# A recurrent loop fed by streamed weights: homes for resident weights opened earlier, the ring filled ahead of the loop, kept outputs stored by partition

## The chip, the cores and the metric

The kernel runs on one core of a Trainium2 chip. The metric is the device time of one execution in microseconds. Three executions of the kernel before took 2130.72, 2140.69 and 2147.24 us; their median is 2140.69 us. A fourth execution was profiled.

## What is computed

Two independent results stand side by side in the output, columns 0 to 1023 (part A) and 1024 to 2047 (part B), both over 2048 rows in bfloat16.

```python
# A: a short causal convolution, a product, a long convolution by FFT, a gate
k_shift = sum(k_pad[:, t:t + S, :] * shift_k[:, ks - 1 - t] for t in range(ks))   # ks = 4
kv = k_shift * v
y = irfft(rfft(kv, 2 * S) * rfft(ssm_k, 2 * S))[:, :S, :] + kv * ssm_D
a = q * y
# B: attention with a recurrent memory, 64 segments of 32 rows, H = 32 heads of 128, M = 8
mem = mem0
for s in range(64):
    h = concatenate([mem, x[:, 32 * s:32 * s + 32]], axis=1)        # 40 rows
    q, k, v = h @ Wq, h @ Wk, h @ Wv                                # [32 heads, 40, 128]
    p = softmax(where(mask, q @ k.T * scale, -1e9))
    o = (p @ v) @ Wo
    mem = o[:, :8]                                                  # into the next segment
    outs.append(o[:, 8:])
```

Each segment needs all of Wq, Wk, Wv and Wo (8 MB each, 32 MB together), which is more than SBUF holds, and needs the memory rows that the segment before it has put out.

## The kernel before, in words

**Order.** Everything is written in one function under a manual schedule: each engine carries out its instructions in the order in which the program gives them. Most transfers are issued by SP, in order, and an SP instruction that waits holds up all that stand behind it; others are issued by ACT and by POOL.

**Part A** is a four-step transform. Stage 1 (to line 510) makes SK1 and SU1 in DRAM. Stage 2 (lines 513 to 620) runs a software pipeline over 17 sets x 2 halves, index `i` from -1 to 34: `load_set` gathers a set of K and U from DRAM, two sets ahead, into buffers of the pool `gio` (three of each); `unit_k`, `unit_u`, `unit_prod` and `unit_back` work on them; `scatter` stores the result to SZ. Stage 3 (lines 623 to 653) takes 16 tiles `t`: it loads `zt` from SZ and `qt`, two tiles ahead, multiplies on PE into `y_ps`, and DVE multiplies by `qt` into `ot`, which SP stores. `ot` has two buffers.

**The row work of part B.** Of the 40 rows of a segment, the last 8 are not touched by the recurrence when q, k and v are formed. The class `Rows` does their projections for all segments at once, in between part A's work, as 192 half steps of four matmuls: 12 units (q, k and v of four head groups) of eight pieces each. A piece is one half, 256 KB, of a weight pair. `rows.load_to(n)` issues the loads of pieces up to n, into the pair's lasting home if it has one (`res_half`), and otherwise into one of the eight tiles of `pring`. Results are gathered in `stq` (q and k, stored to QKBd by ACT after each k unit) and `stv` (v, stored to VBd by POOL).

**Weights.** The 64 pairs [128, 2, 1024] (512 KB each) are 45 resident ones, 2 that are parked in PSUM (`park`, copied to a ring tile in each segment), and 17 that are streamed in each segment through a ring of five tiles (`wring`). Resident homes are opened pool by pool with `open_res(n)` as space comes free, in the order of first use: 9, 10, 3, 12, 2, and the last 9 just ahead of the loop. The Wo pairs come last in that order: 2 of the 11 resident ones are loaded ahead of the loop, 9 in segment 0 (`first_loads`). The streamed pairs of q, k and o are first copied from DRAM to DRAM into a contiguous form, Wst, by `relay` on POOL: ten in stage 2, two after stage 3.

**The loop** (lines 912 to 995) takes the 64 segments one after the other. `qk_part` and `v_part` project the 32 rows that depend on the memory, `tr_a`, `scores`, `softmax`, `blocks` and `pv` are the attention of one head group, and `wo` the projection that gives `yacc`. When PE is done with a streamed pair, `done` issues the load of the one that is five places ahead (`place`). The attention results of the last 8 rows of each segment, OL, aren't needed by the recurrence; POOL stores them to OLd in DRAM, 64 KB for a segment. In the last segment they are loaded back, into the place of early weights (`Wearly`, as `OLs`), after `wo(u0)`, and behind the loop lines 1000 to 1015 project them with all of Wo: four blocks (`sh`, `rq`) of 256 matmuls, each evicted half by ACT and half by DVE and stored by SP.

**Between stage 3 and the loop** (lines 654 to 706) come: `load_h(0)`, the rest of the pieces, the four parked halves (`park_w`, through `pring`; two rounds of transposes each), the two Wo pairs, the two late relays, the rest of the row work from half step 162 on, the closing of the pools of the row work (`cp`), and only then the pool of the ring, with the first five `place()`.

Of the kernel before, what the change touches and what calls it, by code (L numbers as in the profile page):

```python
# [21 lines left out]
def fused_kernel(ctx: ExitStack, tc, q, k, v, shift_k, ssm_k, ssm_D, outa, x, mem0, Wq, Wk, Wv, Wo, outb, n_seg):  # L22
# [11 lines left out]
    nc = tc.nc  # L34
# [16 lines left out]
    QKBd = dram.tile([4, 128, n_seg * 128], BF, name="QKBd")  # L51
    OLd = dram.tile([n_seg, 128, 256], BF, name="OLd")
    VBd = dram.tile([4, 4, n_seg, 8, 256], BF, name="VBd")
# [30 lines left out]
    cp = ExitStack()  # L84
    stq = cp.enter_context(tc.tile_pool(name="b_stq", bufs=1, side="right"))
    stv = cp.enter_context(tc.tile_pool(name="b_stv", bufs=1, side="right"))
    hb = cp.enter_context(tc.tile_pool(name="b_hb", bufs=1, side="right"))
    hTB = hb.tile([128, 8, n_seg * 8], BF, name="hTB")
    pring = cp.enter_context(tc.tile_pool(name="b_pring", bufs=8, side="right"))
    ps_p = cp.enter_context(tc.tile_pool(name="b_ps_p", bufs=2, space=PSUM, side="right"))  # L90
# [422 lines left out]
    with ExitStack() as c2:  # L513
        gio = c2.enter_context(tc.tile_pool(name="a2_io", bufs=3, side="right"))
        wk = c2.enter_context(tc.tile_pool(name="a2_wk", bufs=2, side="right"))
        ps_u = c2.enter_context(tc.tile_pool(name="a2_psu", bufs=2, space=PSUM))
        ps_k = c2.enter_context(tc.tile_pool(name="a2_psk", bufs=2, space=PSUM))
# [85 lines left out]
        for i in range(-1, len(hs) + 1):  # L603
            if 0 <= i < len(hs):
                st, hf = hs[i]
                if hf == 0:
                    load_set(st + 2)
                    zs_of[st] = wk.tile([128, 2, 1024], BF, tag="zs", name="zs", bufs=3)
            if i + 1 < len(hs):
                K_[i + 1] = unit_k(*hs[i + 1])  # L610
            if 0 <= i < len(hs):
                Y_[i] = unit_prod(*hs[i], K_[i], U_[i])
            rows.half(1)
            if i >= 1:
                unit_back(*hs[i - 1], Y_[i - 1], zs_of[hs[i - 1][0]])
            if i + 1 < len(hs):
                U_[i + 1] = unit_u(*hs[i + 1])
            if i >= 16 and i % 2 == 0:
                relay(1)
    ca2.close()  # L620


    with ExitStack() as c3:
        io = c3.enter_context(tc.tile_pool(name="a3_io", bufs=3, side="right"))
        wk = c3.enter_context(tc.tile_pool(name="a3_wk", bufs=2, side="right"))
        ps_big = c3.enter_context(tc.tile_pool(name="a3_ps", bufs=3, space=PSUM))
        open_res(12)
        zts = {}

        def load_z(t):  # L630
            if t < 16:
# [4 lines left out]
                zts[t] = zt, qt  # L636

        load_z(0)
        load_z(1)
        rows.load_to(rows.at // 16 * 8 + 16)  # L640
        rows.go(4)
        for t in range(16):
            load_z(t + 2)
            rows.half(4 if t < 6 else 1)
            zt, qt = zts[t]
            pt = ps_big.tile([128, 1024], F32, tag="big", name="y_ps")
            for hf in range(2):
                for h in range(2):
                    nc.tensor.matmul(pt[:, hf * 512:(hf + 1) * 512], lhsT=G2h[h][:, :],
                                     rhs=zt[:, h, hf * 512:(hf + 1) * 512], start=(h == 0), stop=(h == 1))  # L650
            ot = wk.tile([128, 1024], BF, tag="ot", name="ot")
            nc.vector.tensor_tensor(out=ot[:], in0=pt[:], in1=qt[:], op=ALU.mult)
            nc.sync.dma_start(rows_view(outa, t), ot[:])
    ca.close()
    open_res(2)
    act = cw_.enter_context(tc.tile_pool(name="b_act", bufs=1))
    act2 = cw_.enter_context(tc.tile_pool(name="b_act2", bufs=2))
    n_o = [key for key in resident if key[0] == "o" and key in res_pool]

    def load_h(s):  # L660

        H_ = act.tile([128, 256], BF, tag="qks", name="H")
        if s == 0:
            nc.gpsimd.dma_start(H_[0:32, :], mem0.rearrange("t (dq c) -> (t dq) c", dq=4))
            nc.gpsimd.dma_start(H_[32:128, :], x[0:24].rearrange("t (dq c) -> (t dq) c", dq=4))
        else:
            nc.scalar.dma_start(H_[:], x[32 * s - 8:32 * s + 24].rearrange("t (dq c) -> (t dq) c", dq=4))
        return H_

# [6 lines left out]
    park_s = stv.tile([128, 4, 1024], BF, tag="stv", name="park_s")  # L676
    halves = [(key, n) for key in parked for n in range(2)]
    assert rows.at >= 160
    rows.load_to(96)
    park_w = []  # L680
    for key, n in halves:
        park_w.append(pring.tile([128, 1024], BF, tag="pring", name="park_w"))
        nc.sync.dma_start(park_w[-1][:], half_src(key, n))
    for key in n_o:
        for n in range(2):
            res_half(key, n)
    relay(len(relaid))
    rows.half(6, "AD")
    for i, (key, n) in enumerate(halves):
# [5 lines left out]
        for c in range(8):  # L695
            nc.tensor.transpose(park[key][n][:, c * 128:(c + 1) * 128], park_s[:, i, c * 128:(c + 1) * 128], ident[:])
    while rows.at < 192:
        rows.half(2, "AD")
    assert len(rows.loaded) == 96
    cp.close()  # L700
    ring = cw_.enter_context(tc.tile_pool(name="b_ring", bufs=RING, reuse_waits="tile"))
    open_res(len(to_open))

    pp = ExitStack()
    ps_a = pp.enter_context(tc.tile_pool(name="b_ps_a", bufs=3, space=PSUM))
    ps_ts = pp.enter_context(tc.tile_pool(name="b_ps_ts", bufs=1, space=PSUM))

    placed = {}
    to_copy = []
    todo = [key for s in range(n_seg) for key in streamed if key[0] != "o" or s < n_seg - 1]  # L710

    def place():

        if todo:
            key = todo.pop(0)
            t = ring.tile([128, 2, 1024], BF, tag="wring", name="wring")
            nc.sync.dma_start(t[:], Wst[key])
            placed.setdefault(key, []).append(t[:])

# [6 lines left out]
    def pair(key):  # L726
        return res[key][:, :, :] if key in res else placed[key].pop(0)

# [32 lines left out]
    def qk_out(u):  # L761
        u.qks = act.tile([128, 512], BF, tag="qks", name="qks")
        nc.scalar.copy(u.qks[:], u.qk[:])  # L763
# [23 lines left out]
    def tr_a(u):  # L787
        tp = transposes(u.qks)
        tv = tp[:].rearrange("e (j t c r) -> e t c j r", j=4, t=2, c=2)
        QK = act.tile([128, 8, 72], BF, tag="qks", name="QK")  # L790
        u.QT, u.KT = QK[:, :, 0:32], QK[:, :, 32:72]
# [4 lines left out]
    def load_b(s):  # L796
        qkb = act.tile([128, 4, 128], BF, tag="qkb", name="qkb")
        nc.sync.dma_start(qkb[:], QKBd[:, :, s * 128:(s + 1) * 128].rearrange("g e x -> e g x"))
        return qkb
# [58 lines left out]
    def pv(u, s):  # L858
# [11 lines left out]
        if u.g == 3 and s + 1 < n_seg:  # L870
            nc.gpsimd.dma_start(OLd[s], OL[:].rearrange("e h r -> e (h r)"))

# [29 lines left out]
    def new_hT():  # L902
        return act.tile([128, 8, 32], BF, tag="hT", name="hT")

    for _ in range(RING):
        place()
    load_vb(0)
    qkb = load_b(0)
    n_o = [key for key in resident if key[0] == "o" and key not in n_o]
    hT = new_hT()  # L910
    h_rows(H, hT, 0)
    for s in range(n_seg):
        last = s + 1 == n_seg
        def first_loads(g):
            for key in (n_o[3 * g:3 * g + 3] if s == 0 else ()):
                for n in range(2):
                    res_half(key, n)
# [25 lines left out]
        if last:  # L943
            spare = [key for key in resident if key[0] != "o" and key[1] < 1 + (key[0] == "qk") and key not in early]
            for key, at in zip([key for key in streamed if key[0] == "o"], spare):
                nc.sync.dma_start(res[at][:], Wst[key])
                res[key] = res[at]
        qk_part(u2, range(4, 8))
        qk_out(u2)
# [24 lines left out]
        wo(u0, Y)  # L974
        if last:
            for s0, s1 in ((0, 32), (32, s)):
                nc.sync.dma_start(OLs[:, s0:s1].rearrange("e s h r -> e s (h r)"),
                                  OLd[s0:s1].rearrange("s e x -> e s x"))
        pv(u2, s)
# [20 lines left out]
    for sh in range(2):  # L1000
        for rq in range(2):
            pl = ps_l.tile([128, 1024], F32, tag="pl", name="pl")
            for h in range(32):
                w = pair(("o", h // 8, h % 8 // 2))[:, h % 2, :]
                for hf in range(2):
                    for r in range(4):
                        nc.tensor.matmul(pl[32 * r:32 * r + 32, hf * 512:(hf + 1) * 512],  # L1007
                                         lhsT=OLs[:, 32 * sh:32 * sh + 32, h, 4 * rq + r],
                                         rhs=w[:, hf * 512:(hf + 1) * 512], start=(h == 0), stop=(h == 31),
                                         tile_position=(0, 32 * r))  # L1010
            ol = ring.tile([128, 2, 1024], BF, tag="wring", name="ol")
            nc.scalar.copy(ol[:, 0, 0:512], pl[:, 0:512])
            nc.vector.tensor_copy(ol[:, 0, 512:1024], pl[:, 512:1024])
            for r in range(4):
                nc.sync.dma_start(outl[24 + 4 * rq + r, 32 * sh:32 * sh + 32, :], ol[32 * r:32 * r + 32, 0, :])
    msched.__exit__(None, None, None)
# [67 lines left out]
```

## Time and profile before

| | us |
|---|---|
| three executions, median | 2140.69 (2130.72 to 2147.24) |
| the profiled execution | 2131.23 |
| its span | 2129.3 |
| busy: PE, DVE, ACT, POOL | 1710.2, 1119.4, 919.0, 417.8 |
| stage 2's pipeline, from the first gathers to the last scatter | about 165 to 283 |
| stage 3, to the last store of `ot` | about 286 to 365 |
| loop, from the first `x_tp` to the end of the last `Y_sb` | 400.2 to 2061.3 |
| projection of the kept outputs (`pl`) | 2067.0 to 2124.0 |

Transfers move 728.63 MB in the span, 342 GB/s in the mean. The page of the profile gives, for each engine, its busy time; below that the groups of instructions by line; the chain of waits, which goes back from the last instruction to whatever released it; and the transfers by the line that issues them. `PE` is the matmul part of TensorE, `PEld` its weight loads, `SPq` the issuing of transfers on SP. Views of a single engine list instructions in order of time: start, duration, engine, line, operation, names, count, and in brackets the idle time ahead of an instruction with what ended it. In the views of stretches each line is one stretch: its length, the busy time of PE, PEld, DVE, ACT and POOL (with counts), the granted clock of PE, the busy share of the 16 DMA engines, and GB/s.

### The profile page before, as it was taken

Reading aid. Unit: us, or ns where it says so; the run is one execution under the profiler, and the core shown is the slowest. Engines: PE = TensorE matmul, PEld = TensorE weight load, DVE = VectorE, ACT = ScalarE, POOL = GpSimd, SP = SyncE. Lnnn points to the kernel's source line nnn. Section 1 sums busy time; section 2 is a strip of 40 time slices with the busy share of each in tenths; the row PEclk is TensorE's granted clock in tenths of the full one; section 3 lists DMA queues with packets and bytes.
Section 4 is the critical chain, followed back from the end, with each engine's and each line's share of the span. In section 5 each row is a group of like instructions: output and inputs, shape, how many; then the busy total and the mean of one; then the engine's idle time right before and its main releaser. Section 6 shows DMA issues by size and latency. Waiting matters only on the chain.

```text
span 2129.3 us, 74034 instructions
## 1 busy us (share of the span) xinstructions
PE 1710.2 (80%) x30514; PEld 893.4 (42%) x30514; DVE 1119.4 (53%) x3364; ACT 919.0 (43%) x2282; POOL 417.8 (20%) x1023
## 2 busy tenths in 40 slices
PE   5888976778887788887888888887888787888879
PEld 3332222334444444444444444444444444444448
DVE  7986823235555555555555555555555555555530
ACT  5556731234444444444444444444444444444430
POOL 3004730011111111111211111111111121111110
PEclk9999989899999999999999999999999999999999
DMA  7799979799999999999999999999999999999990
GB/s 271 261 337 338 321 259 354 269 344 372 373 365 352 355 375 369 359 363 369 367 375 354 368 378 350 369 358 362 374 363 365 369 359 373 353 374 355 374 318 22
DMA packets 267375, 728.63 MB, mean 342 GB/s; under 512 B 64751, under 2 KB 75903, under 8 KB 266525
## 3 DMA queue, kind: packets, MB, share of 16 engines
q1 hardware_dynamic: 241294, 687.24, 87.8%
q0 software_dynamic: 15520, 22.06, 3.3%
q10 hardware_dynamic: 10224, 14.62, 1.9%
q8 instruction: 239, 3.92, 0.7%
q14 instruction: 98, 0.80, 0.1%
HBM read 673.52 MB, written 56.56 MB: 343 GB/s over the span
## 4 chain that ended last, share of the span: by engine, by line
DMA 48%; PE 32%; DVE 9%; ACT 5%; issue 3%; SPq 1%; POOL 0%; ACTq 0%; DVEq 0%; POOLq 0%
DMA wring<-in_B_Wv_dram 20%; DMA wring<-Wsto 12%; PE qkacc L757 10%; DMA wring<-Wstqk 9%; PE vacc L771 4%; PE yacc L878 3%; PE pl L1007 3%; PE tp L784 2%; PE ps_v L178 2%; PE ps_q L181 2%; PE otacc L863 2%; PE ps_k L181 1%; DMA out_dram<-ot 1%; DVE PB L856 1%; ACT qks L763 1%
## 5 line engine op out<-in xcount | busy, mean ns | idle before, releaser
L757 PE MATMUL qkacc<-Wqk,hT 128*32 128x512 bf16 x4096 | 337.5, 382 | 0.0
L757 PEld LDWEIGHTS <-hT 128*32 128x32 bf16 x8192 | 186.3, 96 | 237.4 <-issue 85.9
L878 PEld LDWEIGHTS <-OT 128*32 128x32 bf16 x8192 | 210.0, 96 | 110.1 <-issue 59.1
L878 PE MATMUL yacc<-Wo,OT 128*32 128x256 bf16 x5632 | 237.6, 274 | 17.5 <-ACT OT L867 15.2
L757 PE MATMUL qkacc<-wring,hT 128*32 128x512 bf16 x2048 | 207.2, 393 | 29.0 <-DMA wring<-Wstqk 24.1
L771 PE MATMUL vacc<-wring,hT 128*32 128x512 bf16 x1536 | 144.2, 390 | 99.2 <-DMA wring<-in_B_Wv_dram 97.5
L724 DVE COPY wring<-park 128x1024 bf16<-128x1024 bf16 x128 | 88.5, 692 | 242.7 <-PE vacc L771 161.6
L771 PE MATMUL vacc<-Wv,hT 128*32 128x512 bf16 x2560 | 210.6, 383 | 0.0
L837 ACT ACTIVATE P<-S 128x128 bf16<-128x128 f32 x256 | 70.9, 277 | 318.5 <-DVE S L829 228.8
L771 PEld LDWEIGHTS <-hT 128*32 128x32 bf16 x4096 | 111.8, 96 | 223.4 <-issue 149.4
L793 ACT COPY QK<-tp 128x256 bf16<-128x256 bf16 x256 | 95.2, 372 | 231.0 <-PE tp L784 231.0
L792 POOL COPY QK<-qkb 128x64 bf16<-128x64 bf16 x256 | 61.1, 239 | 635.5 <-PE tp L784 467.6
L757 PE MATMUL qkacc<-Wearly,hT 128*32 128x512 bf16 x2048 | 166.9, 404 | 18.5 <-DVE hT L898 17.9
L856 DVE COPY PB<-P 32x160 bf16<-32x160 bf16 x896 | 173.4, 194 | 10.6
L723 ACT COPY wring<-park 128x1024 bf16<-128x1024 bf16 x128 | 130.8, 1022 | 105.0 <-PE qkacc L757 101.3
L841 DVE TENSOR_REDUCE sm<-P 128x4 f32<-128x256 bf16 x256 | 107.5, 420 | 127.7 <-ACT P L838 127.7
L763 ACT CAST qks<-qkacc 128x512 bf16<-128x512 f32 x256 | 150.9, 589 | 20.9 <-PE qkacc L757 14.2
L878 PE MATMUL yacc<-wring,OT 128*32 128x256 bf16 x2520 | 126.2, 274 | 36.2 <-DMA wring<-Wsto 35.0
L867 ACT CAST OT<-otacc 128x256 bf16<-128x256 f32 x256 | 98.9, 386 | 122.0 <-PE otacc L863 122.0
L993 POOL DMA_DIRECT2D out_dram<-Y_sb x256 | 128.6, 509 | 92.3 <-ACT Y_sb L989 90.1
L828 DVE TENSOR_REDUCE mx<-S 128x4 f32<-128x160 f32 x256 | 83.1, 325 | 102.5 <-PE S L825 97.1
L784 PE MATMUL tp<-ident,qks 128*128 128x128 bf16 x1024 | 102.0, 222 | 42.2 <-ACT qks L763 40.2
(216 smaller groups left out, 2818.6 us busy)
## 6 DMA issues: line engine op xcount, KB each, us to landing
wring<-Wstqk SPq DMA_DIRECT2D x448, 512.0 KB, 6.2
wring<-in_B_Wv_dram SPq DMA_DIRECT2D x320, 512.0 KB, 6.7
wring<-Wsto SPq DMA_DIRECT2D x315, 512.0 KB, 6.1
SK<-s_sb SPq DMA_DIRECT2D x8, 1024.0 KB, 5.5
SU<-s_sb SPq DMA_DIRECT2D x8, 1024.0 KB, 6.4
QKBd<-stq ACTq DMA_DIRECT2D x4, 2048.0 KB, 10.2
Kg<-SK SPq DMA_DIRECT2D x16, 512.0 KB, 6.9
Ug<-SU SPq DMA_DIRECT2D x16, 512.0 KB, 6.9
```

The lines of the kernel that those rows point to most:

```text
L723: nc.scalar.copy(t[:, 0, :], park[key][0][:])
L724: nc.vector.tensor_copy(t[:, 1, :], park[key][1][:])
L757: nc.tensor.matmul(u.qk[p0:p0 + 32, :], lhsT=hT[:, kc, :], rhs=w[:, t, c2 * 512:(c2 + 1) * 512], start=(kc == 0), stop=(kc == 7), tile_pos ...
L763: nc.scalar.copy(u.qks[:], u.qk[:])
L771: nc.tensor.matmul(vacc[0][32 * c:32 * c + 32, :].rearrange("p (n x) -> p n x", n=2), lhsT=hT[:, kc, :], rhs=w[:, :, c * 256:(c + 1) * 256 ...
L784: nc.tensor.transpose(tp[:, j * 128:(j + 1) * 128], src[:, j * 128:(j + 1) * 128], ident[:])
L793: nc.scalar.copy(u.QT.rearrange("e (c j) r -> e c j r", c=2), tv[:, 0])
L841: nc.vector.tensor_reduce(out=sm[:], in_=Pv.rearrange("p b x k -> p x b k"), op=ALU.add, axis=AX.XY)
L856: (nc.vector if by[c] == "D" else nc.gpsimd).tensor_copy(to, src)
L867: nc.scalar.copy(u.OT[:].rearrange("e (c i) q -> e i c q", i=2), ov[:, :, :, 0:32])
L878: nc.tensor.matmul(Y[32 * dq:32 * dq + 32, 0:256], lhsT=u.OT[:, hh, 0:32], rhs=w[:, hh % 2, dq * 256:(dq + 1) * 256], start=(u.g == 0 and ...
L993: nc.gpsimd.dma_start(outb[32 * s:32 * s + 24, dq * 256:(dq + 1) * 256], Y_sb[32 * dq + 8:32 * dq + 32, :])
```

## The change

In the order of the program:

- OLd is laid out by partition, [128, segment, 256]; the two loads of the last segment read 16 KB rows of it, and stand in the program behind the loads of the reloaded Wo pairs, ahead of `qk_part(u2, 4..8)`.
- The pools of `stq` and `pring` are no longer closed with the row work; their tiles become homes of seven or eight Wo pairs (`homes`, `Wlate`; `Two` lets a pair lie in two tiles).
- `gio` is closed two half sets ahead of the end of stage 2's pipeline; six homes are opened in its place, and pieces 64 to 71 are loaded at once. Stage 3 opens the other six.
- Relays start at i = 12 instead of 16, so that all 12 are issued in stage 2.
- The last pieces and the four parked halves are loaded at t = 14 of stage 3 instead of after it.
- The pool of the ring, and that of the loop's small tiles that the first steps need (`acte`), are opened right after stage 3, and the ring is filled there.
- Of the 11 resident Wo pairs 7 are loaded during the rest of the row work, an eighth right behind it, and one each at three places of segment 0.
- The last projection runs its column halves one after the other, each with its own accumulator; DVE evicts both, SP and ACT issue two of the four stores each.

```diff
-    OLd = dram.tile([n_seg, 128, 256], BF, name="OLd")
+    OLd = dram.tile([128, n_seg, 256], BF, name="OLd")
...
-    stq = cp.enter_context(tc.tile_pool(name="b_stq", bufs=1, side="right"))
+    stq = cw_.enter_context(tc.tile_pool(name="b_stq", bufs=1, side="right"))
+    pring = cw_.enter_context(tc.tile_pool(name="b_pring", bufs=8, side="right"))
...
-            if i >= 16 and i % 2 == 0:
+            if i >= 12 and i % 2 == 0:
                 relay(1)
+            if i + 2 == len(hs):
+                cg.close()
+                open_res(6)
+                rows.load_to(72)
...
-        open_res(12)
+        open_res(6)
...
             nc.vector.tensor_tensor(out=ot[:], in0=pt[:], in1=qt[:], op=ALU.mult)
+            if t == 14:
+                rows.load_to(96)
+                for key, n in halves:
+                    park_w.append(pring.tile([128, 1024], BF, tag="pring", name="park_w"))
+                    nc.sync.dma_start(park_w[-1][:], half_src(key, n))
             nc.sync.dma_start(rows_view(outa, t), ot[:])
     ca.close()
-    open_res(2)
...
+    ring = cw_.enter_context(tc.tile_pool(name="b_ring", bufs=RING, reuse_waits="tile"))
+    acte = cw_.enter_context(tc.tile_pool(name="b_acte", bufs=1))
...
+    for _ in range(RING):
+        place()
+    homes = [pring.tile([128, 1024], BF, tag="pring", name="Wop") for _ in range(8)]
+
+    def home_o(key, t):
+        res[key] = Two(t)
         for n in range(2):
-            res_half(key, n)
-    relay(len(relaid))
+            nc.sync.dma_start(t[n], half_src(key, n))
...
+    assert rows.at == 176
+    for j, key in enumerate(late_o[:3]):
+        home_o(key, [homes[i][:] for i in ((0, 1), (4, 5), (6, 7))[j]])
+    Wlate = stq.tile([128, 4, 2, 1024], BF, tag="stq", name="Wlate")
+    for j, key in enumerate(late_o[3:7]):
+        home_o(key, [Wlate[:, j, n, :] for n in range(2)])
     while rows.at < 192:
         rows.half(2, "AD")
     cp.close()
-    ring = cw_.enter_context(tc.tile_pool(name="b_ring", bufs=RING, reuse_waits="tile"))
-    open_res(len(to_open))
+    for key in late_o[:8]:
+        to_open.remove(key)
+    n_o = late_o[8:]
+    open_res(3)
...
-            nc.gpsimd.dma_start(OLd[s], OL[:].rearrange("e h r -> e (h r)"))
+            nc.gpsimd.dma_start(OLd[:, s], OL[:].rearrange("e h r -> e (h r)"))
...
-    for _ in range(RING):
-        place()
     load_vb(0)
     qkb = load_b(0)
+    home_o(late_o[7], [homes[i][:] for i in (2, 3)])
...
-            for key in (n_o[3 * g:3 * g + 3] if s == 0 else ()):
+            for key in (n_o[g - 1:g] if s == 0 and g else ()):
...
+            for s0, s1 in ((0, 32), (32, s)):
+                nc.sync.dma_start(OLs[:, s0:s1].rearrange("e s h r -> e (s h r)"),
+                                  OLd[:, s0:s1].rearrange("e s x -> e (s x)"))
         qk_part(u2, range(4, 8))
...
-            pl = ps_l.tile([128, 1024], F32, tag="pl", name="pl")
-            for h in range(32):
-                w = pair(("o", h // 8, h % 8 // 2))[:, h % 2, :]
-                for hf in range(2):
+            for hf in range(2):
+                pl = ps_l.tile([128, 512], F32, tag="pl", name="pl")
+                for h in range(32):
+                    w = pair(("o", h // 8, h % 8 // 2))
...
-            ol = ring.tile([128, 2, 1024], BF, tag="wring", name="ol")
-            nc.scalar.copy(ol[:, 0, 0:512], pl[:, 0:512])
-            nc.vector.tensor_copy(ol[:, 0, 512:1024], pl[:, 512:1024])
-            for r in range(4):
-                nc.sync.dma_start(outl[24 + 4 * rq + r, 32 * sh:32 * sh + 32, :], ol[32 * r:32 * r + 32, 0, :])
+                ol = ring.tile([128, 2, 1024], BF, tag="wring", name="ol")
+                nc.vector.tensor_copy(ol[:, 0, 0:512], pl[:])
+                for r in range(4):
+                    (nc.sync, nc.scalar)[r % 2].dma_start(
+                        outl[24 + 4 * rq + r, 32 * sh:32 * sh + 32, hf * 512:(hf + 1) * 512],
+                        ol[32 * r:32 * r + 32, 0, 0:512])
```

## The prediction

> **What bounds the kernel now.** I read the page's chain of waits first: 48% of it is DMA, 41% the ring loads (`wring`), so the loop waits for weights. I cut the span at the stage borders with the view of stretches (engine busy times, PE clock, DMA share, GB/s).
>
> ```profile
> 278.80:288.30 9.50, 8.58 (x38) 3.48 (x39) 1.42 (x3) 3.51 (x6) 3.28 (x4) 1.00 0.56 184
> 288.30:309.40 21.10, 7.58 (x20) 1.94 (x18) 0.00 (x0) 1.17 (x2) 0.00 (x0) 0.60 0.91 316
> 309.40:366.00 56.60, 44.35 (x200) 18.70 (x199) 20.20 (x17) 9.36 (x16) 3.07 (x4) 1.00 0.99 362
> 366.00:400.20 34.20, 28.63 (x171) 14.61 (x170) 7.71 (x12) 4.10 (x7) 5.45 (x9) 0.95 0.69 242
> 400.20:443.20 43.00, 24.60 (x436) 12.54 (x436) 14.01 (x47) 12.49 (x31) 3.48 (x11) 0.80 0.88 317
> 443.20:472.40 29.20, 22.02 (x436) 11.34 (x436) 13.38 (x46) 11.43 (x32) 4.87 (x14) 0.94 0.94 340
> 472.40:497.50 25.10, 20.63 (x436) 10.89 (x436) 13.47 (x46) 11.35 (x31) 4.88 (x14) 1.00 1.01 369
> 472.40:2060.90 1588.50, 1292.37 (x27030) 685.16 (x27030) 830.80 (x2851) 702.57 (x1922) 301.87 (x867) 0.99 0.99 365
> ```
>
> A normal segment takes 25.1 to 25.6 us at DMA share 0.99: the loop runs at transfer speed, and the change touches none of its bytes. Ahead of it transfers leave time unused (0.56 to 0.94), and segments 0 and 1 take 43.0 and 29.2 us. The timelines of PE and SP say why.
>
> ```profile
> 296.92 0.59 PE L178 MATMUL ps_v<-Wv,hTB 128*128 128x512 bf16 x1 [7.94 <-issue]
> ...
> 372.23 0.62 PE L692 MATMUL park_t<-ident,park_w 128*128 128x128 bf16 x8 [3.94 <-DMA park_w<-in_B_Wv_dram]
> ...
> 418.25 0.62 PE L771 MATMUL vacc<-wring,hT 128*32 128x512 bf16 x4 [9.13 <-DMA wring<-in_B_Wv_dram]
> ...
> 2067.00 3.28 PE L1007 MATMUL pl<-Wo,Wearly 128*32 128x512 bf16 x32 [6.14 <-DMA Wearly<-OLd]
> ```
>
> ```profile
> 265.29 13.48 SPq L534 DMA_DIRECT2D SZ<-zs  x3
> ...
> 288.32 0.43 SPq L119 DMA_DIRECT2D Wv<-in_B_Wv_dram  x1
> ...
> 408.85 2.71 SPq L119 DMA_DIRECT2D Wo<-in_B_Wo_dram  x6
> ...
> 422.20 6.78 SPq L119 DMA_DIRECT2D Wo<-in_B_Wo_dram  x6
> ```
>
> The weights of the next projection are first issued at 288.32, when stage 2 is over, and PE waits. Nine Wo pairs (three times six halves) are issued inside segment 0, between ring loads, and PE waits 9.13 us for a ring load that was issued behind the first six. At the end:
>
> ```profile
> 2124.04 0.58 ACT L1012 CAST ol<-pl 128x512 bf16<-128x512 f32 x1 [13.09 <-PE pl L1007]
> 2124.66 0.69 DVE L1013 CAST ol<-pl 128x512 bf16<-128x512 f32 x1 [12.93 <-ACT ol L1012]
> 2125.37 1.73 SPq L1015 DMA_DIRECT2D out_dram<-ol  x4
> ```
>
> ACT and DVE evict one after the other, then SP issues four stores alone.
>
> **The change part by part.** Since transfers bind from 309 us on, I count in unused transfer time: stretch x (1 - GB/s / 369), with 369 from a normal segment. 4.8 us (278.8 to 288.3), 3.0, 1.1, 11.8 (366 to 400), 6.1 and 2.3: 29.1 us. That is what earlier loads can win at most if no byte goes away.
>
> **Stage 2's input buffers become six pairs' homes.** At i = 32 of the stage 2 loop, eight 256 KB loads (pieces 64 to 71) now follow the last full scatter, issued at 278.8 (end of the 13.48 us row). PE reads the input buffers last at 277.5 (`Uim`), so they are free. Eight issues of at most 0.48 us each take SP to 282.6, just when the last scatter is ready (282.61 before): it and the four z and q loads are moved past by about nothing, 1 us at most. 2.1 MB run where transfers stood at 184 GB/s. PE can go on with `ps_v` at 288.8, not 296.9; then z loads end last. I leave 1.5 us of the 4.8 unused.
>
> **Two relays more inside stage 2** (12 pairs from i = 12 on, before 10 from i = 16). Four POOL issues of 0.52 us each in iterations that keep a 3.07 us step beside a relay (ACT's `Kre` at 256.10, 259.17, 262.24, relay at 257.95), and 1.05 MB between 216 and 228 us, where the DMA share was 0.98 and 0.90. Cost nothing, hidden by gathers two sets ahead; at worst 3 us if they come late. The stretch from 369 on loses 1.05 MB, 2.8 us: 31.9 us to be won.
>
> **Loads at t = 14.** Pieces 92 to 95 and the four parked halves go ahead of the last two `ot` stores: eight issues, 3.6 us by 0.45 each. PE waits for neither store (two `ot` buffers), and the 3.94 us wait for `park_w` goes. What waits is the ring: its homes lie where stage 3's buffers were, so its first load stands on SP until the last store has landed (about 5 us, median 4.9 for `ot`).
>
> **Ring and seven Wo pairs ahead of the loop.** 2.6 + 3.7 MB, 17 us at 369, over some 30 us of row work. But four pairs in `stq` wait for the last `QKBd` store (issued 384.96, 15 us before the loop; such stores take 10.2 us in the median), and SP stands still meanwhile; `qkb` of segment 0 and an eighth pair, which needs the last two ring tiles of the row work, are behind them. Nothing else is: PE's row work has all its weights. I let 5 of the 11.8 us stay unused (between 0, all filled, and 11.8, nothing). Segment 0 then has three pairs to load, not nine, and a full ring: of its 6.1 and segment 1's 2.3 us 1 stays.
>
> Sum: 31.9 - 1.5 - 1.1 (stage 3, as it is) - 5 - 1 = 23.3 us.
>
> **OLd by partition.** The store keeps 64 KB in 128 rows of 512 B, now 32 KB apart. The two loads become 16 KB rows. In the transfer view around the end the rate is 400 to 419 GB/s under the Wsto reloads and 280 to 315 under OLd. The first half is 32 x 64 KB = 2.1 MB: 7.2 us at 293, 5.1 at 410. Their earlier place in the program wins nothing: SP issues them at 2050.26 after the reloads as before, transfers being full. 2.1 us; between 0 (the old rate) and 6.1 (the whole wait).
>
> The Trainium skill's "TensorE: Matmul & The Clock Gate" (Part 1) has the array at half rate after an idle window of about 3.4 us; here 6.14 us of waiting were followed by a clock of 0.53 from 2065 to 2070. With 4 us of waiting left it would still slow down, by a wait shorter than the window some 1.5 us more would be won (32 matmuls took 3.28 us there, 1.8 at the full rate of 57 us for 1024), and the sum would be 2110.
>
> **Last projection.** 1024 matmuls of `pl` before and after; half the accumulator is evicted while the other half runs. After the last matmul one DVE eviction (0.69) and two issues per queue (0.87): 0.62 + 0.87 = 1.5 us less. All ACT evictions become DVE's, hidden by 57 us of matmuls. `Two`, the moved pools and homes issue nothing of their own.
>
> Total: 23.3 + 2.1 + 1.5 = 27 us. The profiled execution took 2131.2 us (span 2129.3 and 1.9 around it): 2104. It is at the fast end of those shown (2130.7, 2140.7, 2147.2); from the mean of all four, 2137.5, the same gain gives 2111 us.
>
> **Rivals.** *Full transfers.* From 309 to 366 the share is 0.99; early loads may only push z loads back, and the ring's head start be eaten by Wo loads. Only the 366 to 400 gap is then won: 11.8 and 3.6 at the end, 2122. For: stage 3's chain goes through `ot` stores of 4.5 to 5.9 us in a full queue. Against: unused time lies ahead of stage 3 too, and segment 0 carries 3.1 MB less.
>
> *The homes are not free.* If the eight loads wait for the last stage 2 work, and `stq`'s four pairs land in segment 0, the loads come no earlier than before: 4.8 + 3.0 and half of 11.8 are not won, a gain of about 13, 2124. For: SP stood 6.8 us at 296 for a `QKBd` store. Against: PE's last reads at 277.5.
>
> *OLd's store.* Rows 32 KB apart may cost transfer time in each of 63 segments of a loop that has none to spare. Now 64 KB cost 0.22 us at 293 GB/s. To be slower by 1% it must eat 27 + 21 us: from 0.76 us per segment on, 4.5 times today's cost; at five times (0.88 us) 2111 + 55 = 2166. Against: `zt<-SZ` reads rows 64 KB apart and lands in 6.5 us, ring loads of the same 512 KB in 6.1 to 6.7; `qkb` reads 512 rows 16 KB apart in 5.0.
>
> The Trainium skill's "DMA: Bandwidth & Descriptors" (Latency and other measured facts) reports copies slowed by row pitches that are large powers of two, 207 GB/s at 512 KiB. By that figure the two OLd loads would take 20 us in place of 14, and the sum would be 2117 with no OLd gain, an estimate; no run here has such a pitch, and the rows of `zt` speak against it at 64 KB.
>
> **How the numbers follow.** Forecast 0.70 (gain 18 to 36: 31.9 with all filled and 3.6 at the end), full transfers 0.12, homes 0.09, the store 0.09. A measurement tells 1%, 21 us, from no change: below 2119 is faster. Of the forecast 0.64 is below, 0.06 above; of the homes 0.02 below and 0.07 above; full transfers within; of the store 0.08 slower, 0.01 within. Faster 0.66, same 0.26, slower 0.08. The range takes gains of 36 and 12 from 2137.5, 2101 and 2125, and the scatter of the runs (about 7 us either way): 2094 to 2132. The forecast's own range is 2096 to 2120.
>
> **What would show it.** Right: `Wv` loads issued near 279 and no PE wait at 297; no `park_w` wait; segment 0 near 27 us, segment 1 near 25.6; `pl` starting some 4 us after the last `yacc` matmul, not 6.1; a normal segment unchanged. Wrong: DMA share below 0.8 still between stage 3 and the loop, segment 0 above 35 us, or a normal segment above 25.9, by which 63 segments would take back 19 us.

## The result, and the profile after

The changed kernel takes 2113.55 us in the median of six executions (2106.34 to 2124.30), the kernel before 2137.80 us beside it; the ratio is 0.9884, with a 95% interval from 0.9841 to 0.9927. The forecast was 2111 us, and faster by 27 us; it became 24. A second set of six executions of the same kernel had a median of 2107.78 us (ratio 0.9868, 0.9841 to 0.9896). All twelve together have a median of 2110.7 us.

The profiled execution took 2120.15 us, its span is 2118.4 us. The view of stretches, cut at the same places in the program as before (length, busy time of PE, PEld, DVE, ACT and POOL, PE clock, DMA share, GB/s):

```profile
278.20:286.00 7.80, 6.83 (x30) 2.77 (x30) 1.27 (x3) 2.93 (x5) 3.28 (x4) 1.00 0.97 323
286.00:300.00 14.00, 8.19 (x32) 3.18 (x31) 0.14 (x1) 2.34 (x4) 0.81 (x1) 0.87 0.97 347
300.00:357.00 57.00, 44.42 (x191) 18.45 (x194) 20.06 (x17) 8.79 (x15) 3.35 (x5) 0.97 1.04 387
357.00:385.90 28.90, 26.72 (x167) 13.87 (x170) 7.51 (x11) 4.10 (x7) 2.30 (x3) 1.00 0.94 345
385.90:420.30 34.40, 22.28 (x436) 11.32 (x436) 13.88 (x47) 12.31 (x32) 3.58 (x11) 0.90 0.86 313
420.30:446.00 25.70, 20.92 (x438) 11.27 (x438) 13.38 (x46) 11.65 (x32) 4.92 (x14) 1.00 1.00 367
446.00:2051.00 1605.00, 1301.25 (x27014) 684.62 (x27016) 831.60 (x2851) 702.33 (x1921) 303.12 (x867) 0.98 0.99 361
```

Transfers now run at 0.94 or more from 278 us up to the loop, and segment 1 is a normal one. Segment 0 with 34.4 us is not: a share of 0.86 is left in it. The timeline of SP shows the loads where the change puts them:

```profile
278.23 0.35 SPq L119 DMA_DIRECT2D Wv<-in_B_Wv_dram  x1
...
284.22 0.32 SPq L541 DMA_DIRECT2D SZ<-zs  x1
290.36 0.57 SPq L638 DMA_DIRECT2D zt<-SZ  x1
...
363.62 6.36 SPq L714 DMA_DIRECT2D Wop<-in_B_Wo_dram  x6
379.24 3.83 SPq L714 DMA_DIRECT2D Wlate<-in_B_Wo_dram  x8
```

The first `Wv` load is issued ten microseconds earlier than before. The last scatter (L541) is 1.6 us later, behind the eight early loads, and the first z load 4.5 us later: it reads what the scatters store, and SP waits 5.8 us for the last of them to land, where it waited 2.7. From 370 to 379 us SP waits for the QKBd store out of `stq`. The timeline of PE answers to the four waits of before:

```profile
288.06 0.38 PE L178 MATMUL ps_v<-Wv,hTB 128*128 128x512 bf16 x1
...
297.79 1.89 PE L656 MATMUL y_ps<-zt,G2h 128*128 128x512 bf16 x4 [5.52 <-DMA zt<-SZ]
...
359.11 0.61 PE L722 MATMUL park_t<-ident,park_w 128*128 128x128 bf16 x8
...
392.44 1.05 PE L784 MATMUL qkacc<-Wearly,hT 128*32 128x512 bf16 x8 [6.24 <-DVE hT L917]
...
2056.68 2.00 PE L1031 MATMUL pl<-Wop,Wearly 128*32 128x512 bf16 x16 [5.01 <-DMA Wearly<-OLd]
```

The waits for `Wv` and `park_w` are gone; a wait for z is in place of the first. New is the fourth line: the loop's first `qkacc` waits 6.24 us for a DVE copy. The timeline of DVE there:

```profile
385.09 0.69 DVE L156 CAST stv<-ps_v 128x512 bf16<-128x512 f32 x1 [2.76 <-PE ps_v L178]
391.78 0.33 DVE L768 MEMSET PB<- 128x320 uint32 x1 [6.01 <-DMA VBd<-stv]
392.02 0.36 DVE L917 COPY hT<-x_tp 128x256 bf16<-128x256 bf16 x1
```

and the same place in the kernel before:

```profile
400.10 0.33 DVE L741 MEMSET PB<- 128x320 uint32 x1
400.59 0.42 DVE L890 COPY hT<-x_tp 128x256 bf16<-128x256 bf16 x1 [0.17 <-PE x_tp L889]
```

PB lies in the pool `act`, which used to be opened right after stage 3. Now it is opened behind the end of the row work, when `cp.close()` has given `stv` free:

```diff
     ca.close()
...
-    act = cw_.enter_context(tc.tile_pool(name="b_act", bufs=1))
...
     cp.close()
...
+    act = cw_.enter_context(tc.tile_pool(name="b_act", bufs=1))
```

DVE's wait in front of the clearing of PB ends with the last VBd store, which reads `stv`, so PB lies where `stv` lay (this is concluded from the wait; no view shows an address). DVE takes its instructions in order, and the copy that PE needs is next. So this wait comes from the place of the line that opens a pool.

### The profile page after: what moved, and what is told of

The parts are those of the page before. It is cut to its first block, busy times and chain, and to the rows that moved or that the text cites. A ratio compares the mean times of both kernels' runs of the same rounds, so it can differ in the third digit from the quotient of the medians.

```text
span 2118.4 us, 74044 instructions
## 1 busy us (share of the span) xinstructions
PE 1714.0 (81%) x30484; PEld 892.0 (42%) x30514; DVE 1123.4 (53%) x3368; ACT 916.2 (43%) x2278; POOL 419.3 (20%) x1023
## 4 chain that ended last, share of the span: by engine, by line
DMA 47%; PE 31%; DVE 10%; ACT 6%; issue 3%; SPq 1%; POOL 0%; ACTq 0%; DVEq 0%; POOLq 0%
DMA wring<-in_B_Wv_dram 20%; DMA wring<-Wsto 10%; PE qkacc L784 9%; DMA wring<-Wstqk 9%; PE vacc L798 4%; PE yacc L905 3%; PE pl L1031 3%; PE tp L811 2%; PE ps_v L178 2%; PE otacc L890 2%; DVE PB L883 2%; PE ps_k L181 1%; PE ps_q L181 1%; DVE S L856 1%; DVE mx L855 1%
## 5 line engine op out<-in xcount | busy, mean ns | idle before, releaser
L820 ACT COPY QK<-tp 128x256 bf16<-128x256 bf16 x256 | 95.4, 373 | 227.6 <-PE tp L811 226.5
L1017 POOL DMA_DIRECT2D out_dram<-Y_sb x256 | 129.1, 511 | 86.8 <-ACT Y_sb L1013 84.5
L890 PE MATMUL otacc<-PB,vsb 128*128 128x160 bf16 x512 | 97.9, 238 | 35.9 <-ACT vsb L805 35.9
```

What stands on the lines that cost most here:

```text
L890: nc.tensor.matmul(o, lhsT=w[:, i * 128:(i + 1) * 128], rhs=PB[:, 2 * kb + i].rearrange("p c q -> p (c q)"), start=(kb == 0), stop=(kb == 1))
L1017: nc.gpsimd.dma_start(outb[32 * s:32 * s + 24, dq * 256:(dq + 1) * 256], Y_sb[32 * dq + 8:32 * dq + 32, :])
```

## The experiments

Single executions of one kernel differ by some 7 us (one standard deviation, both kernels), so a part worth 3 us isn't seen in the time of a few of them. Each experiment is therefore read at two landmarks of its profile too: when SP begins to issue the last `ot` store (the end of stage 3), and the stretch from there to the end of segment 1 (the start of the evacuation into its `Y_sb`). The expectations count this stretch from the row in which SP issues the last two `ot` stores, 0.7 to 1.2 us earlier in most profiles. The table also has the mean of segments 2 to 63 and the stretch from the last `Y_sb` to the first `pl`, all in us.

The ratios are taken to executions of the kernel before that ran beside each kernel, in four series with medians of 2137.80, 2138.50, 2137.31 and 2133.61 us. So medians of two series can differ by some us though the kernels are the same.

| kernel | last `ot` | to the end of segment 1 | mean segment | to first `pl` | median time (executions) | ratio to before (interval) |
|---|---|---|---|---|---|---|
| before | 365.4 | 107.0 | 25.62 | 6.1 | 2137.80 (6) | 1 |
| changed | 356.5 | 89.0 | 25.91 | 4.9 | 2113.55 (6) | 0.9884 (0.9841 to 0.9927) |
| changed, again | 361.3 | 91.6 | 25.69 | 3.8 | 2107.78 (6) | 0.9868 (0.9841 to 0.9896) |
| OLd by segment | 358.9 | 92.2 | 25.58 | 6.1 | 2115.39 (6) | 0.9891 (0.9865 to 0.9917) |
| homes late | 366.1 | 88.8 | 25.68 | 4.1 | 2117.08 (4) | 0.9911 (0.9879 to 0.9942) |
| ring late | 358.8 | 92.7 | 25.60 | 4.2 | 2110.90 (4) | 0.9878 (0.9847 to 0.9909) |
| Wo late | 356.8 | 96.8 | 25.75 | 3.8 | 2122.34 (4) | 0.9927 (0.9898 to 0.9956) |
| parked halves late | 356.6 | 95.4 | 25.70 | 4.1 | 2115.07 (5) | 0.9912 (0.9874 to 0.9949) |
| relays late | 358.4 | 93.9 | 25.68 | 3.8 | 2110.72 (6) | 0.9892 (0.9858 to 0.9926) |
| PB on POOL | 359.8 | 84.5 | 25.70 | 4.0 | 2105.34 (5) | 0.9854 (0.9829 to 0.9880) |
| PB on POOL, again | 360.0 | 84.4 | 25.73 | 3.8 | 2105.99 (6) | 0.9865 (0.9825 to 0.9906) |
| PB on POOL, ring late | 359.4 | 88.7 | 25.67 | 3.8 | 2107.60 (9) | 0.9891 (0.9857 to 0.9925) |
| PB on POOL, `load_to(68)` (same order of transfers) | 359.0 | 83.3 | 25.63 | 3.8 | 2100.36 (4) | 0.9848 (0.9795 to 0.9902) |
| before, the edits at the end alone | 365.6 | 107.1 | 25.50 | 3.8 | 2129.65 (10) | 0.9973 (0.9943 to 1.0004) |

The theory was the prediction's: loads moved into unused transfer time ahead of segment 2 win the time, and the loop stays as it is. The first pair of profiles spoke for it and against it at once: the end of segment 1 came 27.0 us earlier (472.4 to 445.4), more than the 23.3 of the sum, but the mean segment was 25.91 us instead of 25.62, which over 62 segments takes back 18, and is just above the 25.9 that the prediction names as a sign of being wrong. The first rival was therefore the store to rows 32 KB apart.

**OLd by segment.** The changed kernel with the old layout; the store and the two loads follow it.

```diff
-    OLd = dram.tile([128, n_seg, 256], BF, name="OLd")
+    OLd = dram.tile([n_seg, 128, 256], BF, name="OLd")
```

> The changed kernel with OLd kept by segment as before (one 64 KB block for a segment, 512 B rows when it is loaded back). Loads ahead of the loop win the time (theory): the end of segment 1 stays at 445 us of the span, the mean of segments 2 to 63 stays at 25.6 to 25.9 us within 0.15, pl starts 6 us after the last yacc instead of 5, and the time is 1 to 3 us longer, near 2116. The store to rows 32 KB apart slows every segment (rival): the mean segment falls by the 0.29 us that the two profiles differ by (25.91 against 25.62), 18 us in all, and the time goes to about 2097.

The mean segment was 25.58 us, which looks like the rival; the time was not, 2115.39 in place of 2097. The second profile of the changed kernel (25.69) and the ten other profiles with the new layout (25.50 to 25.75) show that 25.91 belonged to one execution. The rival of 0.3 us a segment falls. What the layout does is seen at the end: `pl` waits 6.1 us again.

**The yardstick.** The changed kernel once more.

> The changed kernel once more, as a yardstick for how far the landmarks of one profile scatter (end of segment 1 at 445.4 us in its first profile, 451.2 and 451.5 in two kernels that differ from it only behind that point or in the ring's filling). Theory (the ledger of unused transfer time, 23.3 us ahead of segment 2): 448 to 451 here, time 2112 to 2116. Rival (the 27.0 us of the first two profiles are the true size): 444 to 447.

The end of segment 1 came at 452.8 us, later than either expected. Of three kernels that are the same up to there (with the old layout's 451.2) the mean is 449.8; the kernel before, which has a second sample in the last row of the table, has 472.4 and 472.6. The part ahead of segment 2 is thus worth 22.7 us, give or take some 2, and 27.0 was a lucky profile. The end of segment 1 in a single profile scatters by about 4 us (one standard deviation of the three), the stretch behind stage 3 by about 1.7.

**Homes late.** Without the step at i = 32; `gio` is closed behind stage 2's loop instead, and stage 3 opens all twelve homes.

```diff
-            if i + 2 == len(hs):
-                cg.close()
-                open_res(6)
-                rows.load_to(72)
```

> The changed kernel without the step at i = 32: all twelve homes are opened in stage 3 again, pieces 64 to 71 are loaded behind the first z loads. Theory (idle transfer time at 278 to 288 is what this part wins): the end of segment 1 goes from 445 to 451 to 453 us, PE waits for Wv near 297 again, the time is 6 to 8 us longer, near 2121. Rival (stage 3 runs at transfer speed anyway, and the early loads only push the z loads back): stage 3 ends where it ends now, at 356 to 357 us, and the time stays within 3 us of 2114.

Stage 3 ends at 366.1 us, where it ended before (365.4), against a mean of 358.7 in the eleven profiles that load early: 7.4 us. In the timeline of PE the old wait is back:

```profile
296.25 0.58 PE L178 MATMUL ps_v<-Wv,hTB 128*128 128x512 bf16 x1 [6.18 <-issue]
...
301.98 0.58 PE L178 MATMUL ps_v<-Wv,hTB 128*128 128x512 bf16 x1 [3.26 <-DMA Wv<-in_B_Wv_dram]
```

The rival (early loads only push z back) falls at this landmark. At the end of segment 1, 454.9 us, 5.0 of the 7.4 are left, within the scatter. The median is 3.5 us above the changed kernel's first and 6.4 above its twelve, where 6 to 8 were expected.

**Wo late.** The eight Wo pairs keep their homes, their loads go into segment 0.

```diff
-        for n in range(2):
-            nc.sync.dma_start(t[n], half_src(key, n))
+        later.append((key, t))
...
+            for key, t in (later[3 * g:3 * g + 3] if s == 0 else ()):
+                for n in range(2):
+                    nc.sync.dma_start(t[n], half_src(key, n))
```

> The changed kernel with the loads of the seven Wo pairs and the eighth moved from the row work into segment 0 (three pairs at each of the first places, as before); homes as they are. Theory: 4.2 MB, 11 us at 369 GB/s, are moved, some 3 to 5 us of it into the idle stretch at 386 to 396: the end of segment 1 goes from 445 to 451 to 454, the time to about 2121. Rival (the Wo loads are hidden behind PE's work in either place): 445 to 447.

The stretch behind stage 3 is 96.8 us, 5.9 more than the mean of its three samples (90.9), 3.7 of it left at the end of segment 1, and the time is 2122.34, the longest of all changed kernels. The theory stands; segment 0 takes 42.2 us, against 34.4 in the changed kernel and 43.0 before.

**Ring late.** The five first `place()` behind the row work.

```diff
-    for _ in range(RING):
-        place()
     homes = [pring.tile([128, 1024], BF, tag="pring", name="Wop") for _ in range(8)]
...
+    for _ in range(RING):
+        place()
     load_vb(0)
```

> The changed kernel with the ring's first five loads issued just ahead of the loop, behind the row work, as before; the pool stays where it is. Theory: 2.6 MB, 7 us at 369 GB/s, go from the row work into segment 0, the end of segment 1 moves from 445 to 450 to 452. Rival (there is room for them at 386 to 396 us, where DVE waits for a VBd store and transfers stand at a share of about 0.4): 445 to 447, no change in the time.

The end of segment 1 was 451.5 us, and the time 2110.90. The 450 to 452 of the theory were counted from 445; against the yardstick's mean of 449.8 it is 1.7 later, within the scatter. The ring's loads run while PE stands still for PB: 411 GB/s from 388.4 to 395.6 us, where the changed kernel makes 257 from 385.9 to 392.4. This speaks for the rival: filling the ring ahead of the loop wins little in the changed kernel.

**Parked halves late, and relays late.** In the one the last pieces and `park_w` are loaded behind stage 3, in the other relays start at i = 16 and two are left for later.

```diff
-            if t == 14:
-                rows.load_to(96)
-                for key, n in halves:
-                    park_w.append(pring.tile([128, 1024], BF, tag="pring", name="park_w"))
-                    nc.sync.dma_start(park_w[-1][:], half_src(key, n))
...
     ca.close()
+    rows.load_to(96)
+    for key, n in halves:
+        park_w.append(pring.tile([128, 1024], BF, tag="pring", name="park_w"))
+        nc.sync.dma_start(park_w[-1][:], half_src(key, n))
```

> The changed kernel with the last pieces and the four parked halves loaded behind stage 3, as before, ahead of the ring. Theory: PE's wait for park_w (3.94 us before the change) is back, the rest of the row work and the loop's start are 3 to 4 us later, the time near 2117. Rival (transfers bind, their order is of no matter): the loop's start moves, but the end of segment 1 and the time stay within 2 us.

```diff
-            if i >= 12 and i % 2 == 0:
+            if i >= 16 and i % 2 == 0:
                 relay(1)
...
+    relay(len(relaid))
```

> The changed kernel with relays from i = 16 on, so that two pairs are copied behind stage 3 again. Theory: 1.05 MB, 2.8 us, go back into a stretch whose transfer share is 0.94: the end of segment 1 is 2 to 3 us later, the time near 2116. Rival (the two extra relays hold up stage 2's gathers, 3 us at worst): stage 2 ends earlier by 1 to 3 us and the time does not rise.

With the halves late PE waits for them again, 3.72 us, and the stretch behind stage 3 is 95.4, 4.4 more. But eight loads, 2.1 MB, have moved from ahead of the last `ot` store into this stretch; at the end of segment 1 (452.0) 2.1 us are left, which the rival allows, so the size of this part stays open. With the relays late the stretch is 93.9, 3.0 more, and stage 3 ends at 358.4, no earlier than the others: the two extra relays cost stage 2 nothing that can be seen. Both medians lie near the changed kernel's, so both sizes rest on one profile each, and the relays' 3.0 is less than twice the scatter of that stretch.

**PB on POOL.** The new wait, taken off DVE: POOL, whose next instruction needs the same VBd store anyway, clears PB.

```diff
-    nc.vector.memset(PB[:], 0.0)
+    nc.gpsimd.memset(PB[:], 0.0)
```

> The changed kernel with the clearing of PB moved from DVE to POOL. In the changed kernel DVE waits 6.01 us in front of it for the last VBd store, whose buffer lies where PB now is, and the first hT copy stands behind it. Theory (this new wait costs what PE stands still for it): first qkacc right behind x_tp, 0.8 us instead of 6.5, the end of segment 1 about 5 us earlier, the time near 2109. Rival (segment 0 is bound by its transfers, and PE only waits for the ring instead): PE starts earlier, the end of segment 1 moves by less than 2 us, the time stays at 2114.

> The changed kernel with PB cleared on POOL, once more, since its 2.4 us against the changed kernel of the same call was smaller than the 6.4 us by which the stretch from the last ot store to the end of segment 1 became shorter. Theory (the 6.4 us stay won, the loop behind it is the same): 85 to 86 us for that stretch again, and a median 5 to 6 us under the 2110 of the changed kernel's twelve runs, 2104 to 2106. Rival (the loop, bound by transfers, takes part of it back): 85 us for the stretch, 2108 to 2110 for the time.

In the timeline of POOL the clearing now waits for the store, as `VB<-VBd` behind it did before:

```profile
389.70 0.75 POOL L191 DMA_DIRECT2D VBd<-stv  x1 [2.70 <-issue]
395.16 0.64 POOL L768 MEMSET PB<- 128x640 bf16 x1 [4.70 <-DMA VBd<-stv]
395.73 0.56 POOL L835 DMA_DIRECT2D VB<-VBd  x1
396.28 0.25 POOL L819 COPY QK<-qkb 128x64 bf16<-128x64 bf16 x1
```

and PE starts the loop 0.84 us behind `x_tp`:

```profile
389.33 0.27 PE L916 MATMUL x_tp<-ident,H 128*128 128x128 bf16 x2 [0.88 <-DVE stv L156]
390.17 0.62 PE L784 MATMUL qkacc<-Wearly,hT 128*32 128x512 bf16 x8 [0.57 <-DVE hT L917]
...
396.58 0.23 PE L847 MATMUL S<-QK 128*32 128x40 bf16 x8 [2.21 <-POOL QK L819]
```

The stretch behind stage 3 is 84.5 and 84.4 us, 6.5 less than 90.9: the wait was on the path. A part of it is only moved, since PE now stands at L847 for a copy that POOL makes behind the same store, 2.21 us here and 3.69 in the second profile. The eleven executions of the two have a median of 2105.3 us, 5.4 under the changed kernel's 2110.7; but six of them belong to the series with the lowest median before, and the intervals of the ratio (0.9829 to 0.9880 and 0.9825 to 0.9906) overlap those of the changed kernel. In the time the gain is not shown.

**PB on POOL and the ring late.**

> PB cleared on POOL and the ring filled only behind the row work. Theory (the ring's early filling won nothing because PE stood still for PB and transfers had that time; with the wait gone it counts): the stretch from the last ot store to the end of segment 1 grows from 85 to 90 to 92 us, 7 us for 2.6 MB at 369 GB/s less what idles. Rival (transfers between stage 3 and the loop are full either way): 85 to 87 us.

88.7 us, 4.2 more than the 84.4 of the two samples. With the wait gone PE meets the late ring loads in segment 0, the first of them with

```profile
392.56 0.40 PE L782 MATMUL qkacc<-wring,hT 128*32 128x512 bf16 x4 [2.25 <-DMA wring<-Wstqk]
```

where neither the late ring in the changed kernel nor the early ring with PB on POOL shows a wait of PE for the ring in the first 20 us of the loop. So PE's standing still had covered the late ring. That the early ring then wins some 4 us rests on one profile; the medians, 2107.60 and 2105.99 in one series, are too close to show it.

**Four pieces, then z.** `rows.load_to(68)` at i = 32, in the kernel with PB on POOL; the other four were meant to come behind the z loads.

> PB cleared on POOL, and only four of the eight early pieces ahead of the last scatter and the first z loads, the other four behind the z loads. PE's wait for the first zt (5.5 us in the changed kernel) becomes shorter. Theory (from 286 us on transfers are full, so their order doesn't matter): the last ot store is issued at 356 to 361 us as in the other kernels. Rival (the z loads that were pushed back set stage 3's end): 352 to 354 us.

The edit does not do this. `rows.half` loads a few pieces ahead by itself (`load_to` at its end), so the next half steps issue the four, and SP still has eight loads between 279.08 and 284.36 us, ahead of the last scatter:

```profile
282.86 1.50 SPq L119 DMA_DIRECT2D Wv<-in_B_Wv_dram  x2
285.05 0.33 SPq L541 DMA_DIRECT2D SZ<-zs  x1
```

```profile
298.68 1.89 PE L656 MATMUL y_ps<-zt,G2h 128*128 128x512 bf16 x4 [5.64 <-DMA zt<-SZ]
```

In the whole profile SP issues the same transfers in the same order as with PB on POOL, and the wait for the first `zt` did not become shorter. Whether the order of z and the early loads matters was therefore not tested. The row is a third sample of PB on POOL: 83.3 us for the stretch, and 2100.36 us in the median of four executions.

**The edits at the end alone**, in the kernel before.

> The kernel before with the two edits at the end alone: OLd by partition (its loads in the old place) and the last projection by column halves with the stores on two queues. Theory: first pl 4.2 us after the end of the last yacc's evacuation instead of 6.1, the end of the span 1.4 us sooner after the last matmul, the mean segment unchanged (25.6 within 0.15): 3 us in all, near 2134.5. Rival (the store to rows 32 KB apart costs the loop 0.3 us a segment): the mean segment 25.9, near 2153. The end of segment 1 is a second sample of the kernel before: 469 to 475 expected.

The mean segment is 25.50 us with the store to rows 32 KB apart, the lowest of all, though the profiled execution is also the fastest of the ten. No cost of the store can be seen: from the upper end of the ratio's interval (1.0004) and the 2 to 4 us won at the end, it is at most some 0.1 us a segment, an estimate. `pl` starts 3.8 us behind the last `Y_sb`, the time has an interval that holds no change, and a difference of 4 us in the medians.

## Why the prediction was right, and where its parts were not

*The sum ahead of segment 2.* 23.3 us were forecast, 22.7 is the mean of the samples. In the first pair of profiles the bytes from the first early load to the end of segment 1 agree, 60.7 MB before and 59.6 after (rate times length of the rows, the two relays less), so it is time that was won, not traffic. Taking the parts away one by one gives 7.4 (homes, with stage 3's end), 5.9 (Wo), 4.4 (parked halves), 3.0 (relays) and 1.7 (ring), 22.4 in all, but at two landmarks. At the end of segment 1 alone the same five are 5.0, 3.7, 2.1, 2.4 and 1.7, 15 in all, each with a scatter of 4 us. So the whole is shown, and that homes and Wo are parts of it; the division is not. The ledger carries over to the loop because the loop's segments neither win nor lose, as far as their mean shows: it scatters by about 0.1 us, 6 us over 62 segments. Its full rate of 369 GB/s is no ceiling: stage 3 now runs at 387, and why is open.

*Stage 2's homes.* 3.3 us of the first stretch and the 3.0 of the second were counted, 6.3; it was 7.4 at the end of stage 3. PE went on with `ps_v` at 288.06 as forecast. That the last scatter and the z loads are moved past "by about nothing, 1 us at most" was wrong: 1.6 and 4.5 us. The count of SP's issues left out that the first z load waits for the last scatter to land, which now stands behind 2.1 MB, and PE waits 5.52 us for z. What this cost is not shown: no run loads z first and the eight pieces early too.

*The relays and t = 14.* The relays fit, 2.8 against 3.0. For the parked halves PE's wait is the one forecast, 3.94 against 3.72; the 4.4 and 2.1 us at the landmarks leave its worth open.

*Ring and Wo.* Here two errors met. The prediction let 5 us ahead of the loop stay unused, for SP's wait on QKBd, and 1 us in the first segments. By its own count the row work's stretch left 1.9 us (28.9 x (1 - 345/369)) and segment 0 5.2 us (34.4 x (1 - 313/369)). SP did wait, from 370 to 379, but the ring's five loads and six Wo halves, issued ahead of that, and the QKBd store itself kept the transfers busy (349 GB/s from 370.0 to 379.2). What the prediction missed is that "the moved pools and homes issue nothing of their own" isn't the same as waiting for nothing: PB's new place made DVE, and behind it `hT` and PE, wait 6.24 us. So segment 0 was "near 27 us" only from its first `qkacc` on (27.9). SP in turn stood 10.1 us for that `qkacc` before it could load the next ring tile, and the unused time lies there:

```profile
385.90:392.40 6.50, 0.27 (x2) 0.12 (x2) 0.60 (x2) 0.00 (x0) 1.12 (x2) 0.70 0.71 257
392.40:400.00 7.60, 7.05 (x112) 3.03 (x116) 2.04 (x4) 4.15 (x6) 0.57 (x3) 0.81 0.50 145
```

The sum came out right with the unused time in the wrong place: some 3 us too much was left in the row work and some 4 too little in segment 0. That the two cancel is luck.

*OLd.* The term was 2.1 us; 6.1 against 3.8 to 4.2 in all profiles with the new layout but the first (4.9) makes 2. The view of transfers around the end of the changed kernel, 40 slices of 0.625 us from 2040 on, gives the rates:

```profile
GB/s 400 334 243 275 360 393 419 433 393 406 406 419 419 498 478 452 419 446 419 446 393 414 410 433 407 410 423 437 447 226 114 29 27 0 0 0 0 0 0 0
```

The OLd loads, from 2050 us on (the 17th number), run at 393 to 447 GB/s where 512 B rows had made 280 to 315.

*The last projection.* The end behind the last matmul is 1.5 us shorter, as forecast:

```profile
2114.59 0.69 DVE L1035 CAST ol<-pl 128x512 bf16<-128x512 f32 x1 [6.04 <-PE pl L1031]
```

The span ends 3.8 us after that line's start, where it ended 5.3 after ACT's before. But `pl` itself took 57.9 us instead of 57.0, in part by its slow start: the first 40 matmuls took 4.3 us (2056.68 to 2061.00), 2.2 at the full rate. From the first `pl` to the end of the span it is 61.7 us instead of 62.3, and 61.0 to 62.6 in the other profiles with the new end, so most of this term was lost again.

*Rivals.* "Full transfers" falls with the homes-late run in that early loads do win time ahead of stage 3; its second half, that the ring's head start is eaten, holds in the changed kernel as far as 1.7 us can tell. "The homes are not free" falls with the first `Wv` load at 278.23 us and the `Wlate` loads from 379.24 on, ahead of the loop. OLd's store falls, as a cost of 0.3 us or more, with the two runs on the layout.

## What to carry to other kernels

Where a long loop runs at transfer speed, what a change ahead of it can win at most can be counted as unused transfer time of the stretches. How much of it stays unused hangs on single waits, and here two guesses at that erred in opposite directions. When a pool is moved, look up whose place its tiles take and which engine touches them first: an in-order engine that clears a buffer waits for the store that still reads the old one, and everything behind it waits too. A part that wins little beside such a wait may win once the wait is gone, as the late ring suggests, so try it again after each repair.

## What the runs showed of the hardware

No cost of rows 32 KB apart can be seen: 512 B stores to them leave the mean segment at 25.50 to 25.91 us in twelve profiles, against 25.58 and 25.62 with one block per segment, and 16 KB reads from them run at 393 to 447 GB/s. The Trainium skill's "DMA: Bandwidth & Descriptors" (Latency and other measured facts) has copies slowed at pitches of 2 MiB and more (164 GB/s and less, where 214 is full), and hardly at 512 KiB (207). The prediction's estimate from the 207 took it for a slowed rate of loads, which it is not, and without the OLd gain it would come to 2119, not 2117. No run here has such a pitch.

PE is slow after a wait of 3.87 us already: in four profiles the first 16 `pl` matmuls took 2.00 us after it, as after 5.01 us in the first profile of the changed kernel, where 16 later ones take 1.05. In its second profile they took 1.41 after 3.87 us: `pl` starts at 2049.26, and the granted clock was 1.00 up to 2050 and 0.51 from there to 2052 us. This agrees with the idle window of about 3.4 us in the Trainium skill's "TensorE: Matmul & The Clock Gate" (Part 1); no run here shows from which wait on the clock falls.
